# Attention and a two-layer perceptron on one core: more Strassen in layer 1, LayerNorm on ScalarE, and a table in place of a planner

## The chip, the cores and the metric

The kernel runs on one core of a Trainium2 chip. The metric is the device time of one execution in microseconds; the kernel before takes 208.98 us (median of 3 runs, 208.88 to 209.49). Times inside a run come from one profiled execution, whose span is the time from its first to its last instruction. PE is the matrix engine, DVE the vector engine, ACT the scalar engine, POOL the GpSimd engine; SP only issues transfers. PEld is PE's loading of weights.

## The reference

Windowed attention (the first 4 keys, and the last 128 positions) over 4 batches, 8 heads, 768 positions and 64 numbers per head; then, on the joined heads (512 columns), a LayerNorm, a layer of 2048 columns with ReLU and a layer back to 512, added to the LayerNorm's input:

```python
keep = is_sink | in_window                 # pos < 4, or 0 <= i - j < 128
a = softmax(where(keep, q @ k.T / sqrt(64), -1e9))
x = (a @ v), heads joined                  # 3072 x 512
xn = (x - mean(x)) / sqrt(var(x) + 1e-6) * g_ln
out = x + maximum(xn @ w_ch1, 0.0) @ w_ch2
```

## The kernel before, in words

The 3072 rows are 24 tiles of 128; two tiles make a chunk `c` (0 to 11), three chunks a batch. Everything is kept in bf16 except PSUM, the statistics and the output.

*Attention.* `chunk` (line 605) loads q, k and v of a chunk through POOL's queue and transposes them, on PE for the first chunks, by a transposing transfer on SP's queue for the later ones. `attend` (777) makes scores (`sc`), the exponential on ACT (`ex`, 814), and the multiplication with a 0/1 mask on DVE (`mk`, 826); from chunk 5 on, in chunks that are not the first of a batch, one mask of four is made by two selects on POOL (821). A 65th column of ones in v gives the softmax's denominator. `value` (844) multiplies with v (`av`, 854), takes the reciprocal (`rc`, 868), writes x (870), and does the LayerNorm: statistics and their aggregate on DVE (874, 876), `(var + eps)^-0.5` on POOL in two steps (882, 883), the centering and scaling `xc` on DVE (885). `xc` is then transposed to `xnt`, from chunk 2 on by a transfer on SP's queue.

*Layer 1* is in `mlp` (1006). The plain form is eight groups `ph` of eight 256-column matmuls (1027; 128-column ones in chunks 0 and 1, 1020), each followed by a ReLU `rl` from PSUM to `hq` on ACT or DVE (1037, 1039). From chunk 4 on (`PAR["half"]`) the first half of the 2048 columns is done by `halves` (927): Strassen's scheme in its form with seven products (`product`, 950) of eight 128-column matmuls each (958). It needs four differences of the weights, made once (`weight_sums`, 913), four differences of tokens per chunk, made on POOL (938), snapshots `tz` of three products on ACT (969), three totals on DVE (980) with a ReLU each on ACT (983), and one direct ReLU on ACT (1001).

*Layer 2* from chunk 2 on is `wino` (1074), Strassen's scheme over all of layer 2: seven products p1 to p7 of eight 256-column matmuls each (1109), eight sums of `hq` on DVE (1092), and per chunk four `keep` (1123) and four `final` additions on DVE (1130). Its running sum z, the region l1, and the pair l2 and r1 lie in three PSUM banks x, w and y.

*Order.* All of it is emitted as operations with priorities and costs. `Plan.run` (115) is a list scheduler: it places each operation on an engine, at a time and in a buffer, by the costs written with it. The engines then execute their queues in that order. Where PE has nothing to do in the first 24 us, multiplications of a zero tile are put in (1236).

Of the kernel before, what the change touches and what calls it, by code (L numbers as in the profile page):

```python
# [7 lines left out]
FP32 = mybir.dt.float32  # L8
# [56 lines left out]
class Plan:  # L65


    SEM = 0.035
    TO_PE = 0.11
    PE_DRAIN = 0.18  # L70
    SWITCH = 0.095
    LANES = 8
    SHARED = 36.0
    MIXED = 1e9
    DMA_BUSY = {}

# [31 lines left out]
    def lat(self, src, dst):  # L108
        if src.eng == "PE" and src.dma is None:
            return -self.PE_DRAIN if dst == "PE" else self.SEM  # L110
        return self.TO_PE if dst == "PE" else self.SEM

    WINDOW = {"PE": 0.2, "ACT": 0.25, "DVE": 0.25, "POOL": 0.25, "SP": 0.0}

    def run(self):
        free = {"PE": 0.9, "ACT": 0.75, "DVE": 0.9, "POOL": 1.5, "SP": 0.75}
        lanes = {"POOL": [0.0] * self.LANES, "HW": [0.0] * self.LANES}
        n_dma = {"POOL": 0, "HW": 0}
        dma_free = {"POOL": 0.0, "HW": 0.0, "all": 0.0}
        mode = "n"  # L120
        ready = [o for o in self.ops if o.n_wait == 0]
        order = []
        tensor = sorted((o for o in self.ops if "PE" in o.engs), key=lambda o: (o.prio, o.seq))
        while ready:
            while tensor and tensor[0].start is not None:
                tensor.pop(0)
            head = tensor[0] if tensor else None
            cand = {}
            first = min([o.prio for o in ready for b in o.bufs if b.ring == "pair" and b.slot is None], default=1e9)
            for o in ready:  # L130
                if "PE" in o.engs and o is not head and o.prio >= PAR["strict"]:
                    continue
                need = [b for b in o.bufs if b.ring and b.slot is None]
                ok, avail, took = True, 0.0, {}
                for b in need:
                    used = [u for s in took.values() for u in s.units]
                    ss = [s for s in self.rings[b.ring] if not s.held and not any(u in used for u in s.units)
                          and not (s.lent and o.prio > first)]
                    if not ss:
                        ok = False  # L140
                        break
                    since = max([min(s.free_at for s in ss)] + [min(free[e] for e in o.engs) - 0.3])
                    s = min((s for s in ss if s.free_at <= since), key=lambda s: (s.rank, s.free_at))
                    took[b] = s
                    avail = max(avail, s.free_at)
                if not ok:
                    continue
                best = None
                for e, (occ, lat) in o.engs.items():
                    r = max([free[e], o.nb, avail + (self.TO_PE if e == "PE" else self.SEM)]  # L150
                            + [d.end + self.lat(d, e) for d in o.deps])
                    if e == "PE" and o.mode_in != mode:
                        r = max(r, free[e] + self.SWITCH)
                    if o.dma is not None:
                        q = "POOL" if e == "POOL" else "HW"
                        r = max(r, lanes[q][n_dma[q] % self.LANES])
                    if best is None or r + lat < best[0] - 1e-9:
                        best = (r + lat, e, r)
# [1121 lines left out]
```

## Time and profile before

| | |
|---|---|
| median of the runs | 208.98 us |
| span of the profiled execution | 206.6 us |
| PE, DVE, ACT, POOL busy | 199.4, 179.6, 119.7, 118.7 us |
| share of PE in the chain that ended last | 90% |
| granted clock of PE over the span | 1.000 |
| bytes read, written | 27.31 MB, 6.29 MB |

How to read it: a row of grouped instructions has the line, the engine, the operation, the output and the inputs with partitions and elements, the count, then the busy time of the group, the mean time of one in ns, and the time that its engine had been idle just before, with what ended it. A row of the stage table has a window and the busy time of PE, PEld, DVE, ACT and POOL in it. The chain of waits goes back from the last instruction to what released each step.

### The profile page before, as it was taken

The numbers are of one execution on the slowest core, as the hardware profiler recorded it, in microseconds if no ns is written. First come the engines' busy times: TensorE is split into PE (matmuls) and PEld (weight loads), VectorE is DVE, ScalarE is ACT, GpSimd is POOL, SyncE is SP. The second block draws the span as 40 slices with busy tenths as digits, with TensorE's granted clock in tenths as the row PEclk, the third lists the DMA queues.
The fourth block names the chain that finished last, engine by engine and source line by source line (L and its number), as shares of the span: only waits on it lengthen the run. The fifth ranks groups of instructions, "written<-read, shape, count | busy, mean of one in ns | idle before, by whom it ended". The sixth has DMA issues, their size and how long they took to land.

```text
span 206.6 us, 6790 instructions
## 1 busy us (share of the span) xinstructions
PE 199.4 (97%) x2766; PEld 165.6 (80%) x2766; DVE 179.6 (87%) x437; ACT 119.7 (58%) x187; POOL 118.7 (57%) x170
## 2 busy tenths in 40 slices
PE   6888999999999999999999999999999999999994
PEld 2557996674698897898998988988988988988993
DVE  7589769899599899899989989989989989998693
ACT  3649477839555655666486486485486585560620
POOL 7977475279039029959649949968627229125000
PEclk9999999999999999999999999999999999999999
DMA  5999999999999999999999999899976411210302
GB/s 117 146 195 195 197 181 205 199 158 171 186 200 124 124 191 101 121 174 101 175 152 137 113 159 143 109 171 114 194 117 101 128 33 23 106 32 19 108 27 84
DMA packets 101341, 27.55 MB, mean 133 GB/s; under 512 B 89652, under 2 KB 99128, under 8 KB 101304
## 3 DMA queue, kind: packets, MB, share of 16 engines
q0 software_dynamic: 67712, 13.37, 81.7%
q1 hardware_dynamic: 33304, 13.43, 34.1%
q8 instruction: 22, 0.36, 0.7%
q10 hardware_dynamic: 288, 0.26, 0.4%
q14 instruction: 15, 0.12, 0.2%
HBM read 27.31 MB, written 6.29 MB: 163 GB/s over the span
## 4 chain that ended last, share of the span: by engine, by line
PE 90%; DMA 3%; DVE 3%; POOL 2%; issue 0%; DVEq 0%
PE one L1109 31%; PE one L1027 20%; PE one L958 12%; PE one L1058 7%; PE one L1020 7%; PE pair L854 5%; PE pair L802 4%; DMA n4b<-in_q_dram 3%; PE one L672 1%; PE pair L721 1%; POOL nat L626 1%; PE one L714 1%; DVE xnt L907 1%; DVE kq L595 1%; POOL vn L589 0%; DVE st L874 0%
## 5 line engine op out<-in xcount | busy, mean ns | idle before, releaser
L1027 PE MATMUL one<-xnt,w 128*128 128x256 bf16 x384 | 46.8, 273 | 0.0
L814 ACT ACTIVATE pe<-pair 128x1024 bf16<-128x1024 f32 (+1 forms) x40 | 36.3, 963 | 18.2 <-PE pair L802 18.2
L1037 ACT ACTIVATE hq<-one 128x512 bf16<-128x512 f32 x58 | 33.4, 590 | 17.9 <-PE one L1020 9.4
L1027 PEld LDWEIGHTS <-w 128*128 128x128 bf16 x384 | 36.3, 98 | 4.0
L1109 PEld LDWEIGHTS <-hs 128*128 128x128 bf16 x320 | 31.0, 98 | 4.0
L882 POOL TENSOR_SCALAR st<-st 128x1 f32<-128x1 f32 x24 | 6.4, 266 | 44.4 <-DVE rec L868 27.5
L826 DVE TENSOR_TENSOR pe<-pe,mask 128x1024 bf16<-128x1024 bf16 (+1 forms) x35 | 27.1, 799 | 1.6 <-ACT pe L814 1.4
L969 ACT COPY tz<-one 128x512 f32<-128x512 f32 x24 | 13.9, 585 | 20.6 <-PE one L958 19.2
L1109 PEld LDWEIGHTS <-hq 128*128 128x128 bf16 x240 | 22.2, 98 | 4.1 <-issue 0.5
L589 POOL DMA_DIRECT2D vn<-in_v_dram x24 | 21.9, 922 | 2.2 <-DMA w<-in_moe_w_ch_dram 1.2
L983 ACT ACTIVATE hq<-hq 128x512 bf16<-128x512 bf16 x24 | 15.1, 630 | 13.1 <-DVE hq L980 12.6
L1109 PE MATMUL one<-w,hq 128*128 128x256 bf16 x160 | 19.2, 273 | 0.0
L980 DVE TENSOR_TENSOR hq<-one,tz 128x512 bf16<-128x512 f32 x24 | 16.4, 684 | 1.9 <-PE one L958 1.0
L1130 DVE TENSOR_TENSOR ot<-one,tm 128x256 f32<-128x256 f32 x40 | 15.9, 412 | 2.1 <-PE one L1109 1.8
L1123 DVE TENSOR_TENSOR tm<-one,x 128x256 f32<-128x256 f32 x40 | 16.6, 414 | 1.2 <-PE one L1109 1.1
L870 DVE TENSOR_TENSOR x<-pair,rec 128x512 bf16<-128x512 f32 x24 | 16.6, 691 | 0.8
L874 DVE BATCH_NORM_STATS2 st<-x 128x6 f32<-128x512 bf16 x24 | 16.5, 687 | 0.2
L1020 PE MATMUL one<-xnt,w 128*128 128x128 bf16 x256 | 16.0, 219 | 0.5 <-DVE xnt L907 0.5
L687 POOL DMA_DIRECT2D nat<-in_q_dram x16 | 14.2, 893 | 3.7 <-DMA w<-in_moe_w_ch_dram 3.7
L938 POOL TENSOR_TENSOR xt<-xnt 128x256 bf16<-128x256 bf16 x16 | 12.2, 778 | 7.1 <-DMA xnt<-xc 7.0
L687 POOL DMA_DIRECT2D nat<-in_k_dram x16 | 14.8, 928 | 2.4 <-DMA w<-in_moe_w_ch_dram 2.4
L1020 PEld LDWEIGHTS <-w 128*128 128x128 bf16 x256 | 14.6, 98 | 1.6 <-issue 0.8
(130 smaller groups left out, 387.7 us busy)
## 6 DMA issues: line engine op xcount, KB each, us to landing
out_dram<-ot SPq DMA_DIRECT2D x17, 256.0 KB
w<-in_moe_w_ch_dram POOLq DMA_DIRECT2D x8, 512.0 KB, 12.8
vn<-in_v_dram POOLq DMA_DIRECT2D x24, 128.0 KB, 6.9
nat<-in_k_dram POOLq DMA_DIRECT2D x17, 128.0 KB, 4.6
nat<-in_q_dram POOLq DMA_DIRECT2D x17, 128.0 KB, 4.9
out_dram<-ot SPq DMA_DIRECT2D x14, 128.0 KB
kq<-nat SPq DMA_TRANSPOSE x32
xnt<-xc SPq DMA_TRANSPOSE x20
```

The lines of the kernel that those rows point to most:

```text
L589: loads[b * RB + r, "v"] = P.op(f"vld{t}", {"POOL": (0.87, 0.9)}, prio, lambda e: G.dma_start(bv.t[:, :, 0:64], v[b, :, 128 * r:128 * (r + ...
L687: lambda e, nat=nat, ap=ap: G.dma_start(nat.t, ap), writes=[nat], dma=SW if c < 6 else (*SW[:2], PAR["llag"]), after=behind(c, 0 if soon e ...
L814: P.op(f"ex{c}{hp}", {"ACT": act(2 * n)}, d + 0.1 + 0.05 * j, lambda e, pp=pp, pb=pb: nc.scalar.activation(pb.t[:, :, 0:n], pp.t[:, :, 0:n ...
L826: V.tensor_mul(pb.t[:, :, 0:n], pb.t[:, :, 0:n], mm),
L870: P.op(f"x{t}", {"DVE": dve(512)}, d + xo + 0.11, lambda e: V.tensor_tensor(x.t.rearrange("p (a h c) -> p a h c", a=2, c=64), pv()[:, :, : ...
L874: P.op(f"bn{t}", {"DVE": fix(0.60)}, d + xo + 0.12, lambda e: V.bn_stats(st.t[:, 8:14], x.t), reads=[x], writes=[st, mv])
L958: nc.tensor.matmul(b.t[:, 128 * h:128 * h + 128], lhsT=lt[:, kk, 128 * h:128 * h + 128], rhs=rh[:, kk, :], start=first and h == 0 and kk = ...
L1020: nc.tensor.matmul(ph.t[:, 128 * s:128 * s + 128], lhsT=w1[u // 2][:, j, 128 * s:128 * s + 128], rhs=xnt.t[:, j, 128 * (u % 2):128 * (u % ...
L1027: nc.tensor.matmul(ph.t[:, 256 * s:256 * s + 256], lhsT=w1[ht // 4][:, j, 128 * (ht % 4):128 * (ht % 4 + 1)], rhs=xnt.t[:, j, :], start=j ...
L1037: nc.scalar.activation(hg.t[:, u % 4, :], ph.t, AF.Relu)
L1109: nc.tensor.matmul(at(r), lhsT=get(left, g)[:, v, s, :], rhs=rhs, start=first and n == 0, stop=n == 7, skip_group_check=True)
L1123: return P.op(f"tm{name}_{c}", {"DVE": dve(256, 1.14)}, pr - PAR["kp"], lambda e: V.tensor_tensor(tm[name].t, at(r), xs[i].t[:, sl], op=AL ...
```

## The change

*Layer 1.* From chunk 4 on both halves of the 2048 columns go through `halves`, now called for `g` 0 and 1, with weight differences of their own (`weight_sums(g)`, four more sums, and two more `hq` buffers held). The token differences are made once per chunk (`token_sums`), on DVE instead of POOL, and both halves use them. A total and its ReLU become one DVE instruction with two clamps:

```diff
-            o = P.op(f"c{n}_{c}", {"DVE": dve(512, 1.14)}, pr, lambda e: V.tensor_tensor(
-                block(n), banks_[bank].t.rearrange("p (i t) -> p i t", i=4), tz.t.rearrange("p (i t) -> p i t", i=4), op=ALU.add),
-            P.op(f"r{n}_{c}", {"ACT": act(512), "DVE": dve(512, 0.26)} if PAR["rd"] else {"ACT": act(512)}, pr + 0.1, ...
+            o = P.op(f"c{n}_{c}{g}", {"DVE": dve(512, 1.14)}, pr, lambda e: V._custom_dve(
+                dve_ops.TENSOR_ADD_SAT, out=block(n), in0=banks_[bank].t.rearrange("p (i t) -> p i t", i=4),
+                in1=tz.t.rearrange("p (i t) -> p i t", i=4), s0=FMAX, s1=0.0),
...
+        n_st = (c >= PAR["half"]) + (c >= PAR["half2"])
+        tokens = token_sums(c, T) if strassen else None
+        quick = [halves(c, T, g, hq[g], tokens) for g in range(n_st)]
+        for u in range(4 * n_st, NH1 // 2):
```

*LayerNorm.* x is written together with its row sum; the mean, the squares with their row sum, and `(var + eps)^-0.5` as exp(-0.5 ln(.)) are on ACT (the mean's sign on either engine); from chunk 2 on the centering and scaling too; from chunk 3 on the reciprocal as exp(-ln(.)). One table set with both functions is loaded at the start by its number:

```diff
+    P.op("tab", {"ACT": (1.5, 1.6)}, -50, lambda e: (nc.scalar.add_instruction(mybir.InstLoadActFuncSet(
+        name=nc.get_next_instruction_name(), engine=mybir.EngineType.Activation, act_func_set_id=LN_EXP)), ...
...
-        P.op(f"bn{t}", {"DVE": fix(0.60)}, d + xo + 0.12, lambda e: V.bn_stats(st.t[:, 8:14], x.t),
-        P.op(f"ag{t}", {"DVE": fix(0.09)}, d + xo + 0.13, lambda e: V.bn_aggr(st.t[:, 14:16], st.t[:, 8:14]),
-            G.tensor_scalar(st.t[:, 17:18], st.t[:, 15:16], 1e-6, None, op0=ALU.add),
-            G.tensor_tensor(st.t[:, 16:17], st.t[:, 17:18], mhalf, op=ALU.pow)),
+            P.op(f"rl{t}", {"ACT": (0.08, 0.2)}, d + xo + 0.099, lambda e: nc.scalar.activation(
+                rc(), pv()[:, :, 64], AF.Ln), reads=[po], writes=[lnb])
+            P.op(f"rc{t}", {"ACT": (0.08, 0.2)}, d + xo + 0.1, lambda e: nc.scalar.activation(
+                rc(), rc(), AF.Exp, scale=-1.0), reads=[lnb], writes=[rcb])
+        P.op(f"x{t}", {"DVE": fix(0.62)}, d + xo + 0.11, lambda e: V.tensor_tensor_reduce(
+            in1=rc().unsqueeze(2).to_broadcast([128, 8, 64]), scale=1.0, scalar=0.0, op0=ALU.mult, op1=ALU.add,
+            accum_out=st.t[:, 13:14]), reads=[po, rcb], writes=[x, st])
+        P.op(f"sq{t}", {"ACT": (0.63, 0.815)}, d + xo + (0.13 if c >= PAR["wino"] else 5.13), lambda e: nc.scalar.activation(
+            sqs, x.t, AF.Square, bias=col(14), accum_out=col(15)), reads=[x, st, nm], writes=[sq])
+            col(17), col(15), AF.Ln, bias=eps, scale=1.0 / DM), reads=[st, sq, Bc["eps"]], writes=[ln])
+            col(16), col(17), AF.Exp, scale=-0.5), reads=[st, ln], writes=[rs])
+                col(18), col(14), AF.Identity, scale=col(16)), reads=[st, nm, rs], writes=[nr])
+            xc.t, x.t, AF.Identity, bias=col(18), scale=col(16)) if e == "ACT" else V.tensor_scalar(
```

*Attention.* The heads of a value product lie 128 columns apart in PSUM instead of 65. No mask is made on POOL any more (`mkp=()`).

*Layer 2.* l1 moves into bank x beside z, so the scheme has two banks; r1 no longer waits for the addition that reads l2:

```diff
-        bank = {n: Buf(f"bk{n}{c}", "one") for n in "xyw"}
-        reg = {"z": ("x", 0), "l2": ("y", 0), "l1": ("w", 0), "r1": ("y", 256)}
+        bank = {n: Buf(f"bk{n}{c}", "one") for n in "xy"}
+        reg = {"z": ("x", 0), "l2": ("y", 0), "l1": ("x", 256), "r1": ("y", 256)}
...
-        d2 = product(1, "p2", "l1", "a12", 1, lo, True)
+        d2 = product(1, "p2", "l1", "a12", 1, lo, False, [prods["p1"]])
-        d3 = product(6, "p3", "r1", "s4", 1, hi, True, [f2])
+        d3 = product(6, "p3", "r1", "s4", 1, hi, False, [prods["p7"]])
```

The four banks of the two score pairs can also be lent to layers 1 and 2, one at a time.

*Order.* `Plan.run` no longer schedules. A table has one entry per operation in the order of their creation: a letter for the engine (P, A, V, G, S for PE, ACT, DVE, POOL, SP) and a start in hundredths of a microsecond, which is used for the order alone; a second table has the buffers.

```diff
+        table = SCHEDULE.split()
+        for o, entry in zip(self.ops, table):
+            o.eng, o.start = engines[entry[0]], int(entry[1:]) / 100
+        return sorted(self.ops, key=lambda o: (o.start, o.seq))
```

In the table the first load of v stands ahead of POOL's other loads (before it stood behind those of k and q of tile 1); the weight slices of layer 1 are loaded in the order 3, 1, 0, 2, with loads of q, k and v between. The last chunk's eight sums, its seven products with their additions, and its four stores read

```diff
+... V18980 V19487
+V18801 V19351 V19202 V19420 V19453 V19618 P19266 V19384 P19354 V19917 P19561 V19670 P19473 V19583 P19824 V19953 P19649
+V19881 V19758 P19736 V19845 S19965 S20070 S19930 S20000 V17329 P18490 V18618 P19911
```

in the order of creation p1, keep, p2, final, p7, keep, p6, keep, p4, final, p5, final, keep, p3, final; so PE runs p1, p2, p6, p7, p5, p3, p4, and DVE's keep of p1 (V19384) is emitted after p2 (P19354).

More of the change, by code (lines that the diff above doesn't have):

```diff
@@ L207, in pe @@
+PE_DRAIN = 0.18
 def pe(us):
[L208 removed]
+    return {"PE": (us, us + PE_DRAIN)}
 def act(n):
@@ L415 @@
     P.ring("pair", [Slot(pairs[i], f"pair{i}", banks[2 * i:2 * i + 2]) for i in range(2)])
-    P.ring("one", [Slot(ones[i], f"one{i}", [banks[4 + i]]) for i in range(4)])
+    P.ring("one", [Slot(ones[i], f"one{i}", [banks[4 + i]]) for i in range(4)]
+           + [Slot(pairs[i][:, j, :], f"half{i}{j}", [banks[2 * i + j]], 1, True) for i in range(2) for j in range(2)])
     for i in range(3):
@@ L1182 @@
     for c in range(NC):
-        if c == PAR["half"]:
-            weight_sums()
+        for g, n in enumerate(("half", "half2")):
+            if c == PAR[n]:
+                weight_sums(g)
         mlp(c)
```

375 lines of the change are left out of this document (185 added, 190 removed).

## The prediction

> **What bounds the kernel now.** I read the page's busy shares first, then the stage table, the waits of PE, and the chain of waits between 100 and 160 us.
>
> ```profile
> span 206.6 us, 6790 instructions
> PE 199.4 (97%) x2766; PEld 165.6 (80%) x2766; DVE 179.6 (87%) x437; ACT 119.7 (58%) x187; POOL 118.7 (57%) x170
> ```
>
> The profiled span is 206.6 us and the median of the runs 208.98, so 2.4 us lie around the span. I make every sum against 206.6 and add 2.4. A share of 97% is an average; the stages say where it is made (window, length, busy us of PE, PEld, DVE, ACT, POOL, clock, DMA):
>
> ```profile
> 0.00:8.00 8.00, 6.06 (x38) 2.90 (x39) 5.54 (x32) 2.83 (x6) 6.74 (x14) 1.00 1.03 121
> 8.00:16.00 8.00, 6.33 (x116) 4.36 (x114) 5.65 (x13) 4.78 (x5) 6.06 (x9) 1.00 1.43 188
> 16.00:24.00 8.00, 7.42 (x143) 6.68 (x143) 6.83 (x16) 5.84 (x10) 5.46 (x8) 1.00 1.51 196
> 104.00:120.00 16.00, 16.00 (x248) 14.17 (x246) 14.69 (x33) 10.36 (x18) 12.53 (x18) 1.00 1.17 133
> 120.00:136.00 16.00, 16.00 (x245) 14.13 (x243) 14.75 (x34) 10.17 (x17) 13.25 (x18) 1.00 1.20 135
> 192.00:200.00 8.00, 8.00 (x92) 7.32 (x90) 6.86 (x14) 3.79 (x7) 0.00 (x0) 1.00 0.11 36
> 200.00:206.60 6.60, 3.60 (x34) 2.90 (x31) 3.12 (x9) 0.00 (x0) 0.00 (x0) 0.99 0.26 86
> ...
> PE one L1020 <- DVE xnt L907: 0.5, 1, 0.5
> ```
>
> PE is full, at full clock, in every stage from 24 to 200 us. Its idle time is 4.2 us before 24 us (8 - 6.06, 8 - 6.33, 8 - 7.42) and 3.0 after 200. The last line is from the waits of PE: half a microsecond, and no wait of PE after 24 us is longer, except one at the very end. A busy PE could still hide waits in pipelined records, so the chain of waits matters more. Its pieces are start, length and work:
>
> ```profile
> 104.43 0.87 PE one L1027 x8
> 105.75 1.75 PE one L1027 x16
> 108.63 3.60 PE one L1109 x32
> 118.93 0.89 PE one L958 x16
> 153.97 3.60 PE one L1109 x32
> ```
>
> Sixteen matmuls of 256 columns take 1.75 us and sixteen of 128 columns 0.89, so the array runs at its column rate with no holes. The layer 2 of a chunk starts at 108.63, and three chunks later at 153.97: 15.11 us per chunk, all of it PE work. So only fewer PE columns, or a better head or tail, shorten this kernel, while the other engines stay below 15.11 per chunk.
>
> **Layer 1 on PE.** In chunks 4 to 11 the second half of layer 1 loses four plain groups of eight matmuls (1.75 / 2 = 0.875 each, 3.50) and gains seven products of eight 128-column matmuls (0.89 / 2 = 0.445 each, 3.12). That is 0.38 less per chunk and, over eight chunks, **-3.0 us**, all on the path. Attention and layer 2 keep their matmuls. The wider spacing in PSUM (heads 128 columns apart instead of 65) leaves the number of columns alone; I cost it at nothing, with 0.1 either way.
>
> **DVE per chunk.** From the two stages above DVE works (14.69 + 14.75) / 32 x 15.11 = 13.9 us per chunk.
>
> ```profile
> L874 DVE BATCH_NORM_STATS2 st<-x 128x6 f32<-128x512 bf16 x24 | 16.5, 687 | 0.2
> L876 DVE BATCH_NORM_AGGREGATE st<-st 128x2 f32<-128x6 f32 x24 | 4.3, 179 | 0.5
> L868 DVE RECIPROCAL rec<-pair 128x8 f32<-128x8 f32 x24 | 4.5, 189 | 3.7 <-PE pair L854 3.5
> L885 DVE TENSOR_SCALAR xc<-x,st 128x512 bf16<-128x512 bf16 x24 | 10.0, 416 | 4.9 <-POOL st L883 4.7
> L980 DVE TENSOR_TENSOR hq<-one,tz 128x512 bf16<-128x512 f32 x24 | 16.4, 684 | 1.9 <-PE one L958 1.0 <-ACT tz L969 0.4
> L1092 DVE TENSOR_TENSOR hs<-hq 128x512 bf16<-128x512 bf16 x40 | 15.0, 418 | 0.8 <-ACT hq L1037 0.6
> L826 DVE TENSOR_TENSOR pe<-pe,mask 128x1024 bf16<-128x1024 bf16 x23 | 20.4, 908 | 0.7 <-ACT pe L814 0.7
> L1066 DVE SCALAR_TENSOR_TENSOR ot<-one,st,x 128x512 f32<-128x512 f32 x4 | 2.9, 736 | 0.0
> L761 DVE TENSOR_TENSOR pe<-pe,mask 128x1024 bf16<-128x1024 bf16 x4 | 2.6, 682 | 0.0
> ```
>
> Two tiles a chunk lose statistics, their aggregate, the reciprocal and the centering: 2 x (0.687 + 0.179 + 0.189 + 0.416) = 2.94. Three more totals add 3 x 0.684 = 2.05. The four token sums come over from POOL; they are half the size of a layer 2 sum, so each lies between 0.21 and 0.42 and together 0.84 to 1.67. A mask returns from POOL in two chunks of three: 0.45 to 0.61. The same mask multiply takes 682 ns while POOL does no elementwise work (L761) and 908 later, beside POOL's sums and selects, which go: between nothing and -0.45 (three masks, two chunks of three). The fused total with its two clamps streams the operands of the plain add; it lies between L980 and the two-operation L1066, up to 0.05 more each, six times 0.3. The product x with a row sum may take up to 0.21 more per tile (half an L1092) for the sum. DVE then needs 13.85 to 16.0 us per chunk; I take **14.1**, since masks and sums of this kind already run at their lower price where POOL is quiet. That is below PE's new 15.11 - 0.38 = 14.73: no cost on the path.
>
> **ACT per chunk.** Now (10.36 + 10.17) / 32 x 15.11 = 9.7 us.
>
> ```profile
> L983 ACT ACTIVATE hq<-hq 128x512 bf16<-128x512 bf16 x24 | 15.1, 630 | 13.1 <-DVE hq L980 12.6
> L1037 ACT ACTIVATE hq<-one 128x512 bf16<-128x512 f32 x58 | 33.4, 590 | 17.9 <-PE one L1020 9.4 <-PE one L1027 8.5
> L969 ACT COPY tz<-one 128x512 f32<-128x512 f32 x24 | 13.9, 585 | 20.6 <-PE one L958 19.2
> L1190 ACT ACTIVATE w<-w,gt 128x512 bf16<-128x512 bf16 x8 | 5.2, 723 | 0.0
> L830 ACT ACTIVATE ps<-one 128x128 bf16<-128x128 f32 x7 | 2.1, 302 | 0.0
> L481 ACT ACTIVATE one_e<-one_e 128x1 f32<-128x1 f32 x1 | 0.2, 203 | 0.0
> L481 ACT ACT_TABLE_LOAD x1 | 1.3, 1283 | 2.0 <-PEq L1261 2.0
> ```
>
> The separate ReLUs go (3 x 0.63) and four direct ones (4 x 0.59); three snapshots (3 x 0.585) and one direct ReLU (0.59) come: 7.8 left. LayerNorm adds per tile a square with row sum, a normalization and up to six one-column steps (log and exp for the reciprocal, the mean's sign, log and exp for the root, the product). Large steps lie between 0.63 (L983) and 0.72 (L1190, with a column operand), the row sum adds up to one small step, and a small step lies between 0.203 (L481) and 0.302 (L830). A tile thus takes 2.3 (five small steps) to 3.5, and a chunk 7.8 + 4.6 to 7.8 + 6.9, so 12.4 to 14.7. I take **13.4**, mid-way, below 14.73 again. If the cover goes, each microsecond above 14.73 costs one per chunk. What waits behind a late LayerNorm step on ACT is the next exponential or snapshot, then a mask or total on DVE, then PE. POOL loses the root, the sums and the select and only issues loads: it is never late for more than now.
>
> **Head.** Start, length, work:
>
> ```profile
> 3.96 0.90 POOL L589 DMA_DIRECT2D vn<-in_v_dram  x1
> ...
> 10.19 0.42 PE L854 MATMUL pair<-vn,pe 128*128 128x65 bf16 x8 [0.91 <-ACT pe L758]
> ...
> 15.38 0.69 DVE L870 TENSOR_TENSOR x<-pair,rec 128x512 bf16<-128x512 f32 x1
> 16.11 0.69 DVE L874 BATCH_NORM_STATS2 st<-x 128x6 f32<-128x512 bf16 x1
> 18.75 1.05 PE L1020 MATMUL one<-xnt,w 128*128 128x128 bf16 x16 [0.45 <-DVE xnt L907]
> ```
>
> The first value matmul waits for v, whose load POOL issues third; the table puts it first, 1 to 2 us sooner. Statistics and aggregate (0.87) leave the chain from x at 15.38 to layer 1 at 18.75 for a small step. But layer 1 also needs its weight slices, which share the load queue, and the table sends two of the four later than now. So between 0 and -2; I take **-0.7**, nearest to the part of the chain that is surely gone.
>
> **Tail, two banks.** Products p1 and p2 of layer 2 now write halves of one bank, and so do p7 and p3. In the table's last chunk PE runs p1, p2, p6, p7, p5, p3, p4, and DVE's read of p1's result stands behind p2.
>
> ```profile
> L1123 DVE TENSOR_TENSOR tm<-one,x 128x256 f32<-128x256 f32 x40 | 16.6, 414 | 1.2 <-PE one L1109 1.1
> ```
>
> If that read is kept off the bank until p2 is done, p6, which needs it, starts some 0.41 plus two handovers (0.6) late, where now the whole length of a product lies between. If not, nothing: 0 to +0.6 once, since in other chunks other work lies between. I take **+0.6**. [...]
>
> **Sum:** 206.6 - 3.0 - 0.7 + 0.6 = 203.5, and 2.4 around it: **205.9 us**. Its own bounds: -2 in the head instead of -0.7 gives 204.6; 0 in the head and 0.7 us of scattered new waits give 207.3.
>
> **The rivals.**
>
> *The head fills.* Before 24 us PE has 4.2 us idle and runs filler matmuls on top, so a gain of 3.0 instead of 0.7 may be had there: 203.6. For it: the filler shows PE without real work; against it: layer 1 waits for weights on a full load queue, which no order of work makes faster.
>
> *DVE takes the bound, half.* If DVE needs 15.0 per chunk, well above my price, seven tenths of the gain go: 208.98 - 8 x 0.11 - 0.1 = 208.0. For it: only 0.6 us per chunk separate my DVE from PE. Against: in 104 to 136 us PE never waits at 92% DVE.
>
> *DVE takes the bound, wholly* (slower). Place: chunks 4 to 11, the token sums and totals ahead of layer 1 and 2. With most of its upper prices DVE needs 15.7; it decides from 15.11 on, and then adds 8 x 0.6 = 4.7: 206.6 + 4.7 - 0.1 + 2.4 = 213.6.
>
> *The log does not share a table with exp* (the change doesn't do what it says). Each turn would load a table, 1.283 us (L481). At four turns a tile ACT needs 13.4 + 8 x 1.283 = 23.7 us a chunk, about 8.5 more than now; even at two a tile, 18.5, 3.4 more in ten chunks: 243. Against: the change loads one set by number at the start. [...]
>
> **Chances.** Forecast 0.53; head fills 0.15; DVE half 0.17; DVE wholly 0.12; tables 0.03. A measurement can tell 0.3% (0.6 us) from no change, so faster is below 208.35: all of the first two and 0.11 of the third, 0.79. Same takes 0.06, slower 0.15. The range runs from 203.0, inside the filled head, to 209.4, beyond the half-bound DVE, and leaves out 0.05 below and 0.15 above.
>
> **What will show it.** Layer 1: 15.11 per chunk becomes about 14.7, with PE still at 16.00 of 16. DVE: masks near 0.68, no more than 14.1 per chunk. ACT: one table load, small steps near 0.2 to 0.3, 85 to 95% busy in the middle. Tail: a gap of PE of about 0.6 behind p2 in the last chunk. The prediction is wrong if PE shows waits for DVE or ACT in the middle, or if the head ends elsewhere than within 2 us of now.

## The result, and the profile after

The changed kernel takes 223.69 us (median of 4 runs, 219.79 to 226.44) against 209.18 for the kernel before beside it: a ratio of 1.058 (1.050 to 1.067). It is slower; the forecast was 205.9. The four runs scatter by 6.7 us, those of the kernel before by 0.6. The ratio, here and in the table below, compares only the runs within 1.5% of each kernel's fastest one (222.58 and 219.79 us of the changed kernel), so it is not the quotient of the two medians (1.069).

From the page of the changed kernel: span, busy shares, the chain of waits by engine, and the row of the DMA engines' load in 40 slices of 5.5 us.

```profile
span 221.1 us, 7256 instructions
PE 200.7 (91%) x2962; PEld 167.0 (76%) x2962; DVE 177.9 (80%) x464; ACT 150.8 (68%) x339; POOL 63.4 (29%) x80
DMA  6999999999999999997996979995243130230014
PE 54%; DMA 15%; ACT 14%; DVE 9%; issue 4%; SPq 1%; DVEq 0%; ACTq 0%
```

PE was 97% busy and 90% of the chain; now it is 91% busy and 54% of the chain, and 15% of the chain is DMA. Averaged over the span no engine is full; something makes all of them wait. Where, the stage table says (window, length, busy us of PE, PEld, DVE, ACT, POOL, clock, DMA):

```profile
40.00:56.00 16.00, 12.62 (x142) 9.48 (x140) 10.42 (x32) 12.25 (x26) 3.25 (x4) 1.00 1.74 127
72.00:88.00 16.00, 13.78 (x178) 8.99 (x176) 12.77 (x29) 10.21 (x26) 5.99 (x7) 1.00 1.95 160
120.00:136.00 16.00, 15.88 (x271) 14.27 (x269) 14.96 (x38) 14.76 (x37) 6.41 (x9) 1.00 1.25 115
136.00:152.00 16.00, 14.16 (x209) 12.96 (x208) 13.71 (x36) 10.73 (x28) 5.76 (x7) 1.00 1.74 142
152.00:168.00 16.00, 15.12 (x260) 13.49 (x259) 14.11 (x38) 12.35 (x27) 0.00 (x0) 1.00 0.44 113
```

Four windows have holes in PE: 3.4, 2.2, 1.8 and 0.9 us, 8.3 together, where the kernel before had none. In them DVE and ACT are less busy than in 120 to 136 us, where PE is nearly full. So neither of the two is full there. The waits of PE (engine, line, what ended the wait: us in total, times, longest) name the cause:

```profile
PE one L1044 <- DMA xnt<-xc: 3.4, 1, 3.4
PE one L974 <- DMA xnt<-xc: 3.0, 2, 2.2
PE pair L802 <- DMA kq<-nat: 1.8, 1, 1.8
...
PE one L1131 <- DVE tm L1145: 0.5, 1, 0.5
```

The first three are waits for transposing transfers on SP's queue, of LayerNorm's rows (`xnt<-xc`) and of q and k (`kq<-nat`). Together they are 8.2 us, and they end at 49.3, 86.0, 139.0 and 164.7 us, each in one of the four windows, so they account for the 8.3. The pieces of the chain of waits at these places (start, length, what):

```profile
40.73 8.55 DMA xnt<-xc
...
77.21 8.76 DMA xnt<-xc
...
134.05 4.84 DMA kq<-nat
...
160.38 4.27 DMA xnt<-xc
```

A transfer issued at 40.73 us lands 8.6 us later, and layer 1 of chunk 2 starts on its landing. At 160 us, where the DMA row stands at 4 tenths instead of 9, the same transfer takes 4.3. ACT's 14% of the chain lie in part ahead of these transfers: from 35.7 to 39.9 us the chain runs through LayerNorm's steps on ACT.

The kernel before has the same transfer at the same place. In the view of the tile `xnt` from 40 to 60 us its two issues are

```profile
L569 SPq DMA_TRANSPOSE xnt<-xc x2: 1198/1742/2287, 44.5 to 46.8; - x2
```

and its chain of waits there reads

```profile
46.41 2.70 PE one L1058 x12
...
49.54 2.70 PE one L1058 x12
...
52.67 1.83 PE one L1058 x8
54.51 1.75 PE one L1027 x16
```

L1058 is layer 2 of chunks 0 and 1, and L1027 layer 1 of chunk 2, the first user of the tile. From the second issue at 46.8 to that use at 54.3 us (the first L1027 in the view of the tile) lie 7.5 us, with 32 matmuls of layer 2 and two scores in them. These transfers are long as well: in the trace the last count on their semaphores comes 7.7 and 6.6 us after the two issues. (Read in the same way the transfer of 40.73 above takes 8.55 us, as the chain has it.) In the old order other work of PE covered them, with 0.9 us to spare; in the changed order less stands there, and PE ran dry.

The end of the span comes from the chain and the timeline (start, length, engine, line, work, count; in brackets the idle time before it and what ended it):

```profile
208.37 4.54 PE one L1131 x40
...
212.94 1.42 DVE L1152 TENSOR_TENSOR ot<-one,tm 128x256 f32<-128x256 f32 x4 [1.32 <-PE one L1131]
...
213.72 1.30 SPq L1175 DMA_DIRECT2D out_dram<-ot  x3
215.07 2.24 SPq L1180 DMA_DIRECT2D out_dram<-ot  x1
217.41 0.38 SPq L1175 DMA_DIRECT2D out_dram<-ot  x1
217.84 0.45 SPq L1180 DMA_DIRECT2D out_dram<-ot  x1
```

and, of the kernel before, from the same two views:

```profile
199.91 3.51 PE one L1109 x32
...
200.12 4.11 SPq L1154 DMA_DIRECT2D out_dram<-ot  x4
```

Before, the last product ends at 203.42 and the span 3.2 us later. (PE's very last work is a pair of small matmuls that reads a last sum, 0.7 us later: 204.1 us before, 213.6 after. Some figures below count from there.) Its four stores are spread over 200.12 to 204.2. After, the last product ends at 212.91 and the span 8.2 us later: all four last sums stand behind the last product, and six stores start behind the first of these sums, the two L1180 among them being stores of chunk 10's tiles. So of the 14.5 us by which the span grew, **9.5** come before the last product's end and **5.0** behind it.

The 9.5 are more than idle PE alone. The products need fewer columns, as forecast: each of eight chunks loses 32 matmuls of 256 columns and gains 56 of 128. That is 192 of the 196 by which the count of matmuls grows; the other four are multiplications of the zero tile. By the rates of the prediction that is 8 x 0.38 = 3.0 us less work. Yet PE's busy time rose from 199.4 to 200.7 us. So some 4 us of PE's busy time (an estimate: 3.0 + 200.7 - 199.4) are no columns of the products. The multiplications of the zero tile ahead of 24 us make up 1.2 us (29 in 7.13 us instead of 25 in 5.91, in the table of the head below). What the rest is, no view shows: the mean record of a matmul is 273 ns at 256 columns and 219 at 128, as before.

### The profile page after: what moved, and what is told of

It is laid out like the page before. It is cut to its first block, busy times and chain, and to the rows that moved or that the text cites. A ratio compares the mean times of both kernels' runs of the same rounds, so it can differ in the third digit from the quotient of the medians.

```text
span 221.1 us, 7256 instructions
## 1 busy us (share of the span) xinstructions
PE 200.7 (91%) x2962; PEld 167.0 (76%) x2962; DVE 177.9 (80%) x464; ACT 150.8 (68%) x339; POOL 63.4 (29%) x80
## 4 chain that ended last, share of the span: by engine, by line
PE 54%; DMA 15%; ACT 14%; DVE 9%; issue 4%; SPq 1%; DVEq 0%; ACTq 0%
PE one L1131 18%; PE one L974 13%; DMA xnt<-xc 12%; PE one L1037 5%; PE one L1044 4%; PE pair L854 3%; ACT sqs L887 3%; ACT pe L814 2%; ACT xc L898 2%; DMA kq<-nat 2%; PE pair L802 2%; ACT tz L985 2%; DVE x L877 2%; PE pair L974 1%; DVE ot L1152 1%
## 5 line engine op out<-in xcount | busy, mean ns | idle before, releaser
L985 ACT COPY tz<-one 128x512 f32<-128x512 f32 x45 | 25.8, 583 | 14.0 <-PE one L974 8.5
L974 PEld LDWEIGHTS <-hq 128*128 128x128 bf16 x512 | 31.3, 98 | 2.5 <-issue 0.4
L996 DVE CUSTOM_DVE_ANT_0 hq<-one,tz 128x512 bf16<-128x512 f32 x40 | 27.0, 687 | 3.5 <-PE one L974 1.8
L974 PE MATMUL one<-xt,hq 128*128 128x128 bf16 x360 | 26.8, 219 | 0.1
L974 PEld LDWEIGHTS <-w 128*128 128x128 bf16 x384 | 23.4, 98 | 4.5 <-issue 3.7
L1131 PEld LDWEIGHTS <-hq 128*128 128x128 bf16 x240 | 22.4, 98 | 3.4 <-issue 0.7
L877 DVE CUSTOM_DVE_ANT_1 x<-pair,rec 128x512 bf16<-128x512 f32 x24 | 16.5, 689 | 6.1 <-ACT rec L875 5.2
L1113 DVE TENSOR_TENSOR hs<-hq 128x512 bf16<-128x512 bf16 x40 | 16.7, 419 | 1.4 <-ACT hq L1016 1.2
L887 ACT ACTIVATE sqs<-x,st 128x512 bf16<-128x512 bf16 x24 | 17.3, 719 | 0.5
L1044 PEld LDWEIGHTS <-w 128*128 128x128 bf16 x128 | 12.2, 98 | 5.5 <-DMA xnt<-xc 3.9
L898 ACT ACTIVATE xc<-x,st 128x512 bf16<-128x512 bf16 x20 | 16.0, 813 | 0.3
L1044 PE MATMUL one<-xnt,w 128*128 128x256 bf16 x112 | 13.1, 273 | 3.4 <-DMA xnt<-xc 3.4
```

Of the source, the lines that this page charges most:

```text
L877: P.op(f"x{t}", {"DVE": fix(0.62)}, d + xo + 0.11, lambda e: V.tensor_tensor_reduce(out=x.t.rearrange("p (h c) -> p h c", c=64), in0=pv()[ ...
L887: P.op(f"sq{t}", {"ACT": (0.63, 0.815)}, d + xo + (0.13 if c >= PAR["wino"] else 5.13), lambda e: nc.scalar.activation(sqs, x.t, AF.Square ...
L898: P.op(f"xc{t}", {"ACT": (0.537, 0.63)} if on_act else {"DVE": fix(0.33 if scaled else 0.26)}, d + xo + 0.17, lambda e: nc.scalar.activati ...
L974: nc.tensor.matmul(b.t[:, 128 * h:128 * h + 128], lhsT=lt[:, kk, 128 * h:128 * h + 128], rhs=rh[:, kk, :], start=first and h == 0 and kk = ...
L985: o = P.op(f"tz{i}_{c}{g}", {"ACT": act(512)}, T + pos[i - 1] - PAR["tzp"], lambda e: nc.scalar.copy(tz.t, banks_[bank].t), reads=[done], ...
L996: o = P.op(f"c{n}_{c}{g}", {"DVE": dve(512, 1.14)}, pr, lambda e: V._custom_dve(dve_ops.TENSOR_ADD_SAT, out=block(n), in0=banks_[bank].t.r ...
```

## The experiments

Two theories stood against each other. By the first, the order is too tight: the table puts the users of a transposing transfer only a few microseconds behind its issue, and PE has nothing else queued when it lands late. By the second, the engines and banks hold the kernel: the work moved to DVE and ACT, or the two PSUM banks of layer 2. Beside them stood the question whether other loads make the transfers slow, and what the stores at the end cost.

| run | edit | median us | ratio to before (95%) | span us |
|---|---|---|---|---|
| the change | | 223.69 | 1.058 (1.050 to 1.067) | 221.1 |
| e1 | longer leads | 223.01 | 1.068 (1.061 to 1.075) | 220.6 |
| e2 | lighter loads | 222.93 | 1.066 (1.057 to 1.075) | 217.8 |
| e3 | small loads early | 219.83 (one run) | | 218.2 |
| e4 | kernel before, two banks | 212.93 | 1.019 (1.013 to 1.026) | 211.2 |
| e5 | stores early | 221.67 | 1.056 (1.045 to 1.067) | 223.9 |
| e6 | e5 and e3 | 222.29 | 1.063 (1.055 to 1.071) | 218.2 |
| e7 | older rows in layer 1 | 220.03 | 1.050 (1.044 to 1.057) | 219.1 |
| e12 | older q and k | 220.35 | 1.055 (1.050 to 1.061) | 218.5 |
| e8 | both older | 214.00 | 1.023 (1.015 to 1.031) | 211.8 |
| e9 | last sums and stores early | 218.52 | 1.045 (1.039 to 1.052) | 217.0 |
| e10 | e8 and e9 | 210.92 | 1.009 (1.005 to 1.013) | 209.4 |
| e11 | e10 and e3 | 209.88 | 1.006 (1.003 to 1.009) | 208.5 |
| e13 | e11, less DVE work | 209.66 | 1.003 (1.000 to 1.006) | 208.1 |
| e14 | e11, less ACT work | 209.92 | 1.003 (1.000 to 1.006) | 208.4 |

**e1: longer leads.** The same operations, engines and buffers; the table's times from 24 us on are made anew, so that the users of a transposed tile stand 5.5 to 10.6 us behind its transfer instead of 3.4 to 7.7. Two of the 1090 entries that differ, the users of chunk 4's rows:

```diff
-V7810
+V8569
...
-V8084
+V8656
```

> The changed kernel with the same 1228 operations, engines and buffers; only the table's times, and so the order on each engine, are made anew from 24 us on, with the durations and landings that the trace of the changed kernel shows (the transposes of normalised rows counted as landing 7.5 us after issue up to 75 us and 5 to 4 us later). By the table's times the second transpose of a chunk was issued 3.4 to 7.7 us before the chunk's first use; now it is 5.5 to 10.6 us. Theory 1 (the order leaves the transposes too little time, so TensorE waits for rows that have not landed): nearly all of the 14.5 us comes back, 206 to 211 us, and no wait of TensorE for a transpose above 1.5 us in all. Theory 2 (the operations themselves are too much for VectorE and ScalarE, whatever the order): stays at 218 us or more.

It is no faster. A piece of its chain and a stage of its table say why:

```profile
53.17 8.34 DMA kq<-nat
```

```profile
56.00:72.00 16.00, 12.51 (x157) 9.62 (x156) 9.14 (x22) 6.87 (x13) 3.50 (x4) 0.89 1.90 154
```

Remaking the order moved the loads too. Now q and k of chunk 4 land late, and the hole is 3.5 us in 56 to 72 us. PE also waits for DVE for 7.3 us between 24 and 212 us, against 1.0 in the change. So this new order has a late transfer and other waits of its own; the run doesn't show that leads don't matter. No run has the new operations in an order of the old planner, so what the operations and what the table contribute to the late transfers is not parted. What was wanted was a test that takes the waiting away without touching the order (e7, e8).

**e2: lighter loads.** q and k from chunk 6 on, and v from tile 12 on, are loaded for one head of eight.

```diff
+                    few = 1 if c >= 6 else H
-                         lambda e, nat=nat, ap=ap: G.dma_start(nat.t, ap), ...
+                         lambda e, nat=nat, ap=ap, few=few: G.dma_start(nat.t[:, 0:few], ap[:, 0:few]), ...
```

> The changed kernel with its own order; the loads of q and k from chunk 6 on and of v from tile 12 on bring one head of eight, so the rest of those chunks is computed from stale rows. Theory 1 with contention (the transposes land late, 4 to 8 us after issue, because the loads hold the DMA engines): landings after 55 us fall to 1 to 2.5 us, and of the 10 us that the order falls behind after 55 us at least 5 come back: 213 to 218 us. If landing depends on the transposes alone: landings as before and 221 us or more. Theory 2 (VectorE and ScalarE too heavy): 221 us or more, though the landings get shorter.

Stages and the longest wait of PE:

```profile
40.00:56.00 16.00, 12.25 (x121) 8.61 (x122) 9.35 (x25) 10.48 (x21) 2.92 (x5) 0.89 1.77 128
...
136.00:152.00 16.00, 16.00 (x262) 14.51 (x260) 15.42 (x41) 12.46 (x31) 1.77 (x3) 1.00 0.50 96
```

```profile
PE one L1046 <- DMA xnt<-xc: 3.6, 1, 3.6
```

Where the loads are lighter the hole is gone: 16.00 in 136 to 152 us instead of 14.16. Before that, at 40 to 56 us, the loads are as they were and so is the wait. So the loads make the later transposing transfers late. The traces show how: from issue to the last count on the semaphore, the two transfers of chunk 4's rows, issued at 76 to 80 us, take 7.3 and 8.8 us in the change and 3.4 and 2.6 here, and LayerNorm's rows don't come from a load. So the transfers themselves get longer beside the loads. That q and k also come late themselves is not ruled out. The median isn't told apart from the change's. The span of the one profile is 3.3 us shorter.

**e3 and e6: small loads early.** Fifteen small loads of v columns, which the table puts at 40 to 57 us between the transposing transfers on SP's queue, go to 4.5 to 8.7 us; e6 moves stores as e5 does, too.

```diff
-S3992 S5658 S5718 S4082 ...
+S450 S480 S510 S540 ...
```

> The changed kernel with the fifteen small loads of sink values, which the table puts on SyncE's queue at 42 to 64 us between the transposes, moved to 4.5 to 8.7 us, where the kernel before has them. Theory 3 (the small loads hold up the transposes in that queue): 2 us or more come back, below 220.5 us. Theory 1: within 1.5 us of 222.6, since the transposes of chunk 2 are issued ahead of them anyway.

219.83 us in one run: inside the scatter of the changed kernel, so nothing follows from it alone.

> The stores as in the run beside it, and the fifteen small loads of sink values at 4.5 to 8.7 us. The look at the small loads alone gave a span of 218.2 us instead of 221.1, with the last product at 211.2 instead of 213.6 us, within what two runs of the changed kernel differ by. Theory 3 (the small loads hold up the transposes): 1.5 us or more below the run beside it, 215.5 to 218 us. Otherwise: the same within 1 us.

222.29: no effect that can be told apart. Its span is 2.9 us shorter, in the one profile.

**e4: the kernel before, with the two banks alone.**

```diff
-        bank = {n: Buf(f"bk{n}{c}", "one") for n in "xyw"}
-        reg = {..., "l1": ("w", 0), ...}
+        bank = {n: Buf(f"bk{n}{c}", "one") for n in "xy"}
+        reg = {..., "l1": ("x", 256), ...}
-        d2 = product(1, "p2", "l1", "a12", 1, lo, True)
+        d2 = product(1, "p2", "l1", "a12", 1, lo, False, [prods["p1"]])
-        d3 = product(6, "p3", "r1", "s4", 1, hi, True, [f2])
+        d3 = product(6, "p3", "r1", "s4", 1, hi, False, [prods["p7"]])
```

> The kernel before with one part of the change alone: layer 2 in two PSUM banks instead of three. Theory 4 (the two banks cost time): 0.6 us or more above before, ratio 1.003 or more, with the cost behind the last layer 2, where the fourth product waits for the first sum, and the sum of the first waits for the second product. Otherwise: within 0.3 per cent of before.

Slower by 1.9% (1.3 to 2.6), 4.0 us by the ratio. The planner made its order anew around the edit, so the 4.0 us are the price of the edit with the order that came of it. A wait of DVE, one of PE, and two neighbours in the timeline:

```profile
DVE tm L1123 <- PE one L1109: 5.7, 12, 0.8
...
PE one L1109 <- DVE ot L1130: 2.9, 6, 0.6
```

```profile
109.06 1.92 PE L1109 MATMUL one<-w,hq 128*128 128x256 bf16 x16
...
111.01 0.42 DVE L1123 TENSOR_TENSOR tm<-one,x 128x256 f32<-128x256 f32 x1 [0.69 <-PE one L1109]
```

The 16 matmuls are p1 and p2. DVE's read of p1's result starts at 111.01, when p2 ends, and not at 110.0, when p1 does: the read waits for the second product in its bank, with DVE idle for 0.69 us. DVE used to wait 1.1 us there in the whole run. PE in turn waits 2.9 us for the additions that read the shared banks (`ot`) and 0.6 for `tm`; the kernel before has neither. Over the ten chunks that go through `wino`, which the order before runs nearly in one piece, that is 4.0 / 10 = 0.4 us per chunk. In the changed kernel other work lies between the products, and PE waits 0.5 us for `tm` in the whole run.

**e5: stores early.** The stores of tiles 20 and 21 stand right behind their sums, and the last four in the order in which their sums end.

```diff
-S20035 S20105 S19965 S20070 S19930 S20000
+S19347 S19560 S19957 S19993 S19921 S19885
```

> The changed kernel with six of the table's entries altered: the two stores of chunk 10's rows (tiles 20 and 21), which the table puts among the last stores of all, go to SyncE as soon as their sums stand there, and the four stores of the last chunk go in the order of their sums. In the trace of the changed kernel the last product ends at 213.6 us and the span 7.5 us later; before, 2.5 us lie between. Six stores are issued from 213.72 on, and the fourth takes 2.24 us to issue. Theory 5 (5 of the 14.5 us are lost behind the last product, in the stores' place): 3 to 5 us less, 217.5 to 219.5 us, with the span's end 3 to 4.5 us behind the last product. Theory 1 alone (all is lost by late transposes): 222 us, and the end of the span lies 7 us behind the last product as before.

221.67, not told apart from the change. In the profile of e6, which has the same stores, the last product ends at 211.69 and the span at 218.2: 6.5 us behind it instead of 8.2. So by the traces the stores alone bring some 1.7 of the 5.0 us.

**e7, e12, e8: older tiles, in the same order.** The waiting for transposing transfers is taken away by reading what landed a chunk earlier. This takes away more than the transfer: the reader no longer waits for what comes ahead of it either, LayerNorm's steps on ACT for the rows, the load for q and k.

```diff
-        xnt = xnt_b[c]
+        xnt = xnt_b[c - (c >= 2)]
```

> The changed kernel with its own order, but from chunk 2 on layer 1 reads the normalised rows of the chunk before, which have long landed; so it computes layer 1 from the wrong rows, and every transposing transfer still runs as before. Theory 1 (TensorE waits for transposed rows that land late): its gaps at 45 to 49 us, at 83 to 86 us, and most of those after 90 us close; the last product ends at 205 to 208.5 us instead of 213.6, the time is 214 to 217.5 us. Theory 2 (VectorE and ScalarE are too heavy) and theory 6 (the granted clock, the loads on GpSimd's queue): the last product within 2 us of 213.6, 220 us or more.

```diff
-        kq = kq_b[c]
-        kprev = kq_b[c - 1] if R else None
+        kq = kq_b[c - (c >= 4)]
+        kprev = kq_b[c - 1 - (c >= 4)] if R else None
```

> The changed kernel with its own order; from chunk 4 on the scores are computed from the transposed q and k of the chunk before, layer 1 from the right rows. The normalised rows alone brought about 2 us, both together 8. If q and k are the cause and the rows wait only because all is late: 214 to 216 us, as both together. If each hides the other (the two must both be there in time): 219 us or more, and the gain of both together is larger than the sum of the two.

> As the run beside it, and from chunk 4 on the scores are computed from the transposed q and k of the chunk before as well. What the late q and k cost by themselves is the difference: theory 1 as I hold it now has the normalised rows as the main part and q and k as a smaller one (the wait for the fourth transfer of chunk 9 at 134 to 139 us, 1.8 us): 1 to 3 us below the run beside it, 212 to 216 us. If q and k are the main part: 4 us or more below it.

With older rows (e7), two stages and the longest wait of PE:

```profile
40.00:56.00 16.00, 15.75 (x166) 12.08 (x166) 14.25 (x40) 15.38 (x35) 3.34 (x5) 1.00 1.70 129
56.00:72.00 16.00, 13.51 (x171) 10.23 (x170) 9.95 (x24) 6.94 (x16) 5.54 (x7) 0.89 1.70 118
```

```profile
PE pair L802 <- DMA kq<-nat: 4.8, 5, 1.6
```

and with older q and k (e12) the longest wait is

```profile
PE one L1044 <- DMA xnt<-xc: 3.1, 1, 3.1
```

Each cure alone brings little: 1.058 becomes 1.050 and 1.055. With older rows the kernel runs up to the other transfer, and PE's waits for q and k grow from 1.8 to 4.8 us. With older q and k the waits for rows don't grow (3.6 us in all, against 6.4 in the change); why so little time is won there stays open. Both together bring it to 1.023, 7.4 us less than the change by the ratios ((1.0583 - 1.0227) x 209). PE's waits for a transposing transfer are then all gone; the longest wait after 24 us, and the last piece of PE's work on the products (x40, the same as at 208.37 in the change), are

```profile
PE pair L854 <- DVE pe L826: 0.8, 1, 0.8
```

```profile
199.63 4.54 PE one L1131 x40
```

The last product ends 8.7 us earlier than in the change. The two gains don't add: by the ratios they are 0.008 and 0.003 alone and 0.036 together. So most of the price is paid as long as either of the two is late.

**e9: last sums and stores early.** The table has three of the last chunk's four sums earlier, two of them ahead of the end of the last product, and the six stores right behind their sums.

```diff
-S20035 S20105 V19917 V19953 V19881 S19965 S20070 S19930 S20000
+S19347 S19560 V19740 V19881 V19800 S19785 S19926 S19845 S19890
```

> The changed kernel with the table's last entries altered: two of the last chunk's four sums go to VectorE as soon as their products stand there, not behind the last product, and the six last stores go to SyncE as soon as their sums stand there. The span ended 7.5 us behind the last product; with the stores alone moved it was 5.8 us, and before 2.5 us. Theory 5: 3 to 4 us behind the last product, so 3.5 to 4.5 us below the changed kernel, 218 to 219.5 us. If the end hangs on the last product's own sums: 5.5 us or more behind it, 221 us or more.

218.52, ratio 1.045; the stores now read

```profile
206.13 3.21 SPq L1179 DMA_DIRECT2D out_dram<-ot  x2
210.97 2.56 SPq L1174 DMA_DIRECT2D out_dram<-ot  x4
```

Tiles 20 and 21 are stored at 206 us, and the four last stores begin before PE is done. The span ends 4.1 us behind the last work of PE (212.9), against 7.5 in the change (213.6) and 2.5 before (204.1). PE still waits 3.3 us for the rows of chunk 2. Of the 3.4 us that the end gets back the stores make some 1.7 (e6's profile), so the sums make about as much again: a store can't start before its sum, whatever the order on SP.

**e10 and e11: all together.** e10 has the edits of e8 and e9, e11 those of e3 as well.

> The stale rows, q and k of the second run and the moved sums and stores of the third in one kernel. If late transposes and the end account for the loss, they add up: 208 to 212 us, against 209.1 us before. If a loss of another kind is left (VectorE, ScalarE, the two banks): 214 us or more.

> The kernel with stale rows, q and k and with the end moved (210.9 us), and the fifteen small loads of sink values at 4.5 to 8.7 us as well. In the trace of that kernel TensorE's first large gap, at 59 to 67 us, ends on those small loads (the last is issued at 63 us and lands at 65.5, then the sink rows are made and the attention of chunk 3 starts). Theory 3 as it stands now (with the transposes out of the way the small loads are what comes last there): 1 to 2 us less, 209 to 210 us. Otherwise 210.5 us or more.

210.92 and 209.88 us; by the ratios the sums and stores bring 2.9 us on top of e8 ((1.0227 - 1.009) x 209). A stage of e11:

```profile
40.00:56.00 16.00, 15.75 (x166) 12.11 (x166) 14.03 (x39) 15.39 (x35) 3.42 (x5) 1.00 1.80 146
```

With the transfers' waits and the late end taken out, the same operations on the same engines come to 1.009, and with the small loads early as well to 1.006 (1.003 to 1.009). So 0.049 of the 0.058 lies in the first two things, or 10 of 12 us; the 0.003 of the small loads is not clear of the intervals. The ACT load of 15.39 in 16 us stands beside a PE at 15.75. Still this is 1.2 us above the kernel before, and not 3 below it. The end is not all had back: e11's span ends 4.2 us behind PE's last work, that of the kernel before 2.5.

**e13 and e14: what holds the rest.** Over e11, e13 makes the eight sums of `hq` on DVE half as wide from chunk 5 on; e14 makes LayerNorm's squares on ACT over 64 of 512 columns.

```diff
-                    sb[n, g].t, get(x0, g), get(x1, g), op=op),
+                    sb[n, g].t[:, 0:few], get(x0, g)[:, 0:few], get(x1, g)[:, 0:few], op=op),
```

> The kernel with stale rows, q and k, the end moved and the small loads early (209.9 us), and VectorE lightened: from chunk 5 on the eight sums that prepare layer 2 of a chunk make half of their rows each (0.42 us down to about 0.2, so 1.6 us less of VectorE's 14 to 15 us in a chunk). My forecast without any late transfer was 205.9, so 4 us are open. Theory 2 in what is left of it (VectorE, 80 to 85 per cent busy, comes late now and then): 1 us or more less, 207 to 208.9 us. If VectorE hides behind TensorE everywhere: 209.3 to 210.2 us.

```diff
-            sqs, x.t, AF.Square, bias=col(14), accum_out=col(15)), ...
+            sqs[:, 0:64], x.t[:, 0:64], AF.Square, bias=col(14), accum_out=col(15)), ...
```

> The same kernel with ScalarE lightened instead: the squares of LayerNorm are summed over 64 of 512 columns (0.72 us down to about 0.25, so nearly 1 us less of ScalarE's 13 us in a chunk, and a chain of LayerNorm that is as much shorter). Theory 2 for ScalarE: 1 us or more less, 207 to 208.9 us. If ScalarE hides behind TensorE everywhere: 209.3 to 210.2 us. If neither of the two runs moves, the 4 us lie in the order that the table lays down, and in the end of the span.

Both come to 1.003. Against e11's 1.006 that is some 0.5 us, with intervals that overlap. The edits took less away than their expectations had: a sum of `hq` takes 283 ns instead of 418 (1.1 us per chunk), a square 345 instead of 718 (0.7 us). Neither brings the missing 4 us by itself. The two were not lightened together; as with e7 and e12, each could hide the other. Against this stands that in both runs PE is busy for 175 of the 176 us between 24 and 200 us, and the last product still ends at 203.4 and 203.7 us. So hardly any idle PE is left there to win; whether part of the busy time is waiting, no view shows.

None of the kernels is faster than the kernel before, not even those that leave work out.

## Why the prediction was wrong

**The step that failed** is one the sum doesn't have. The prediction counted PE's columns, and compared DVE and ACT with PE chunk by chunk; "each microsecond above 14.73 costs one per chunk" was, but for "0.7 us of scattered new waits" in a bound, the only way in which it let PE wait in the middle. The transposing transfers on SP's queue got no term and no rival, although the change lays a new order of everything around them. Its one sentence on the queues, "POOL ... only issues loads: it is never late for more than now", took the queue of loads and not what follows from it: a load, then a transposing transfer, then a matmul. In the kernel before PE never waited for such a transfer, and the prediction put them at nothing, as if they were cheap. They weren't: they took 6.6 and 7.7 us, and the old order had other PE work over them, as its chain from 46 to 56 us shows. Measured: 8.2 us of waits in the trace, and 7.4 us of time when they are taken out, with what comes ahead of them (e8).

**The end of the span** was taken over unchanged: the sum went from the old span, with the 3.2 us behind its last product in it. The table's last sums and stores were quoted ahead of the prediction, and in them the four last additions stand behind the last product and six stores behind these. Measured: 5.0 us more, of which e9 gets 3.4 back (7.5 to 4.1 behind PE's last work). The 2.4 us that the sum puts around the span is too much by 0.9: each run has 1.5 to 1.7 us between its span and its time (221.1 and 222.58 for the changed kernel).

**DVE and ACT.** Their work was sized well. Groups of the changed kernel:

```profile
L996 DVE CUSTOM_DVE_ANT_0 hq<-one,tz 128x512 bf16<-128x512 f32 x40 | 27.0, 687 | 3.5 <-PE one L974 1.8 <-ACT tz L985 1.5
...
L826 DVE TENSOR_TENSOR pe<-pe,mask 128x1024 bf16<-128x1024 bf16 x28 | 18.9, 683 | 2.2 <-ACT pe L814 2.2
...
L887 ACT ACTIVATE sqs<-x,st 128x512 bf16<-128x512 bf16 x24 | 17.3, 719 | 0.5
L898 ACT ACTIVATE xc<-x,st 128x512 bf16<-128x512 bf16 x20 | 16.0, 813 | 0.3
...
L475 ACT ACT_TABLE_LOAD x1 | 1.3, 1283 | 2.0 <-PEq L1283 2.0
```

The fused total with two clamps takes 687 ns, as the plain add did (684). The masks take 683, the forecast 0.68, with no elementwise work left on POOL. The square takes 719, inside its bounds. Only the centering is dearer than its bound, 813 against 720, which makes 0.2 us per chunk. In 120 to 136 us ACT is busy for 14.76 and DVE for 14.96 of 16 us, with PE at 15.88: neither rival of a full DVE came true. Still, by the prediction's own measure ("the chain of waits matters more") the two are not wholly hidden: this chain runs through ACT from 118.2 to 127.1 us, where the kernel before has PE alone, and ACT and DVE together make 23% of the whole chain instead of 3%. The waits of PE show only 1.0 us for the two between 24 and 212 us. The table is loaded once (1.283 us, in the last row), so the rival of the tables falls.

**Two banks.** The forecast gap of 0.6 behind p2 in the last chunk shows as a wait of 0.5 for `tm`, PE's only wait for one in the whole run. That the read waits for the second product, on which the +0.6 rests, no run had shown when the 0.6 was taken; what the runs show in its place is this 0.5, and in e4 a read that starts at 111.01 us, when the second product ends, with DVE idle for 0.69 us ahead of it. The remark that other chunks have other work between the products holds for the changed kernel and not for the old order.

**The head** didn't come out. PE is busy for 21.35 us before 24 us instead of 19.81, and v's load and the first value matmul come sooner (2.37 instead of 3.96, 9.62 instead of 10.19 us). But the gain went to multiplications of the zero tile. Busy PE before 24 us in layer 1 and in these fillers, in the kernel before (L1020, L1236) and in the changed one (L1037, L1258):

```profile
0.00:24.00 24.00, 5.14 (x80) 4.57 (x80) 1.00 1.32 168
0.00:24.00 24.00, 5.91 (x25) 2.32 (x25) 1.00 1.32 168
...
0.00:24.00 24.00, 4.48 (x71) 4.03 (x71) 1.00 1.33 162
0.00:24.00 24.00, 7.13 (x29) 2.70 (x29) 1.00 1.33 162
```

At 24 us layer 1 has done 71 of its matmuls instead of 80, so the -0.7 was not had; layer 1 is about 0.5 us behind (an estimate: nine matmuls of 128 columns, at 0.89 us for sixteen).

**Layer 1** has the columns forecast, and with all waits for transfers gone PE isn't done earlier: e11's last work on PE ends at 204.3 us, that of the kernel before at 204.1. So the -3.0 and -0.7 are not had in this order even then. e13 and e14 speak against a bound on DVE or ACT alone. Ahead of PE's last work hardly any idle PE is left in these two: the rest lies in the head, and in PE's busy time, which is 199.3 us in e11 and 199.4 before although the products have fewer columns. Whether the order, or DVE and ACT together, makes up for those columns stays open; no run here settles it.

The chances went wrong in the same place. Slower had 0.15, all but a fifth of it for DVE, and the outcome lies outside the range by a cause that none of the rivals names.

## What to carry to other kernels

When a change replaces the order of a full kernel, list for each transfer on which the bound engine depends when it is issued, when it is first used, and which other work the engine has in between. A transfer that never shows in the waits need not be short (6.6 and 7.7 us in the kernel before); it may be covered, and the cover is part of the change. Take the time behind the last product as a term of its own. Don't take a busier PE for progress: count the matmuls that are done by then. When a wait is tested, take away its partner too: two late transfers, each hidden by the other, look harmless one by one (1.050 and 1.055, but 1.023 together, against 1.058).

## What the hardware showed beyond that

*The clock falls behind an idle PE.* In e1 PE is nearly idle from 58 to 62 us (1.02 us busy), and then the granted clock (the column before the last two) goes down, to 0.69 and 0.50 in the next two windows:

```profile
60.00:62.00 2.00, 0.45 (x21) 0.34 (x22) 0.42 (x1) 0.06 (x1) 0.87 (x1) 1.00 1.64 149
62.00:64.00 2.00, 2.00 (x18) 1.56 (x14) 0.00 (x0) 1.88 (x2) 1.29 (x2) 0.69 2.20 160
64.00:66.00 2.00, 1.49 (x9) 0.90 (x7) 1.11 (x3) 0.00 (x0) 0.46 (x1) 0.50 1.73 158
```

From 66 to 68 us it is 0.95, then 1.00. At the end of the span it goes down as well, and not after one fixed time: in the change PE's last work ends at 213.6 us and the clock drops to 0.50 at 218.0, 4.4 us later; in the kernel before the two lie at 204.1 and 206.4, 2.3 us apart. In the change's own profile the wait of 3.4 us at 45 to 49 us left the clock at 1.00 in its window, while e2, with a wait of 3.6 us in the same place, has 0.89 there (and 121 matmuls in 40 to 56 us instead of 142), so much the same hole is followed by a lower clock in one run and not in the other. With landing times that vary, this may be part of the wide scatter of the changed kernel, whose four runs of 219.79, 222.58, 224.8 and 226.44 us have mean granted clocks of 0.992, 0.993, 0.982 and 0.975; that was not tested, and the 0.993 of the profiled run comes from the 3.1 us behind 218.0 alone.

*Stores in a row.* Of the six stores behind the last sums the fourth takes 2.24 us to issue and the last two 0.38 and 0.45; the kernel before issues its four, with gaps, in 4.11 us altogether.
